# The opening stretch of a planned SSD and mixer kernel: the words of its first quarter in another order

## The chip, the core and the metric

The kernel runs on one core of one Trainium2 chip. The metric is the device time of one execution in microseconds (us), the median of several runs; for the kernel before the change it is 217.03 us (three runs, 217.02 to 217.46).

## What is computed

First a state space scan (Mamba2 SSD), over 4 batches of 8 heads with 768 tokens, 32 values a token and 16 state values, in chunks:

```python
for c in range(nc):
    cum = np.cumsum(log_a[:, :, sl], axis=-1)
    M = einsum('bhin,bhjn->bhij', Cc, Bc) * exp(cum_i - cum_j) * causal
    y[:, :, sl] = einsum('bhij,bhjd->bhid', M, xc) + einsum('bhin,bhnd->bhid', Cc, state) * exp(cum)
    state = decay_full * state + sum_j Bc_j * xc_j * decay_from_j
```

Then, for each batch, a mixer on the scan's output x (768 tokens by 256 channels):

```python
u = x + (x.T @ U @ V).T          # U: 768x32, V: 32x768
out = u + relu(u @ w_ch1) @ w_ch2   # 256 -> 1024 -> 256
```

U, V, w_ch1 and w_ch2 arrive as 64-bit numbers and are made 32-bit floats on the chip.

## The kernel before

All work is cut into small steps, and a string, PLANS (lines 36 to 71), says in which order they are recorded. Each step is a word: a letter for the kind of step, and numbers for its place. `follow` (lines 1070 to 1089) reads the words one by one and calls the step's function, and each engine then carries out its instructions in just that order. An engine never passes over a waiting instruction to a later one, so the order of the words is the order of TensorE (PE), VectorE (DVE), ScalarE (ACT), GpSimd (POOL) and of the load queue on SyncE (SP). PLANS[0] loads the first scan inputs; PLANS[1] holds everything else, for all four batches.

**The scan** works on pairs of 128-token blocks, three pairs a batch, twelve in all. In a word of PLANS[1] the pair number counts from batch 1: -3, -2 and -1 are the pairs of batch 0, 0 to 2 of batch 1, 3 to 5 of batch 2, and so on. The words of one pair k, in the order in which they depend on each other:

- B and X load B, C and x of a pair (L loads both). Q (one block) or P (the whole pair) multiplies B and C by decay factors on DVE (`prep`, 471). E or D makes the decayed B for the state (`decayed`, 483; on POOL for batch 0, else on DVE).
- V or T transposes that on PE and copies it out on ACT and DVE (`turning`, 494).
- g multiplies C by B on PE (`gram`, 583). It takes four banks of PSUM, two with the tag x and two with z. m and M apply the causal mask on DVE, for two banks each (`mask`, 597), and so free them.
- s makes what the pair adds to the state, on PE (`state`, 616); it takes the two banks with the tag w, which are free again when u has read them. u carries the state on, four small operations on DVE (`update`, 632), and then a masked copy on POOL or ACT.
- i and j multiply C by the carried state, and n the masked product by x, both on PE (`inter`, 699, and `intra`, 734). For batch 0, j may need a copy of one column on DVE, named settled (666), which waits for the products of i and n recorded before it. y copies the result out on ACT, t and O turn it back to tokens.

**The weights.** Z loads V and U. w0 and w1 load the two halves of the first quarter of w_ch1, w2 to w4 the other quarters, and w5 to w8 the quarters of w_ch2. c makes floats of such a load in three steps with one word each (`to_fp32`, 409): two operations on DVE and one on ACT, one on ACT, three on DVE. c0 is for U and V, c1 and c2 for w0 and w1, c3 to c9 for w2 to w8. R splits a quarter for the later, finer products (`refine`, 447), on ACT and DVE. v spreads U and V on PE and ACT (`spread`, 1012).

**The mixer.** p multiplies the scan's output by U, x by V (four banks at once, x and z), and a.0 and a.1 add the result to the scan's output on DVE, one half of the tokens each. For the first two of the three 256-token blocks of batch 0, products are plain: U1.j.i multiplies block j by quarter i of w_ch1, eight PE instructions (the profile shows 32-bit matmuls as two rows each) and a relu on ACT (`plain`, 864), and four words d1.j multiply by w_ch2 (`down`, 937). U1.0.0 needs a1.0, c1 and c2; U1.j.1 needs c3, and so on up to c5; the first d word of a block needs c6 and c7, the second c8 and c9. The third block and all later batches use the split numbers: S splits the input, f and e multiply by the first weights, h and d follow. f1.2.0 is the first such product.

**What sets the order of loads.** All loads are issued on SP, one after the other, and each of the words B, X, w and L is held until the last DVE operation recorded before it is done (`hold`, 197, and line 1075). A load into a buffer that is used again also waits for its last reader.

F sets how many filler products PE runs at the next bank. There are two PSUM banks with the tag w, three with x and three with z (line 130).

Of the kernel before, what the change touches and what calls it, by code (L numbers as in the profile page):

```python
# [70 lines left out]
}


# [1049 lines left out]
```

## Time and profile before

| | us |
|---|---|
| median of three runs | 217.03 |
| the profiled execution | 214.85 |
| its span, first to last instruction | 213.1 |
| PE busy | 202.6 |
| DVE busy | 172.9 |
| ACT busy | 121.3 |

The prediction sums against the profiled execution; its time is the span and 1.75 us around it. A row of a timeline gives the start, the duration, engine, line, operation, tiles and how many instructions are merged in it, and in brackets the idle time of the engine before it with what ended that. "issue" is idle time for which the profile shows no releaser. Times in the trace run from the start of the span. All DVE instructions carry the line 177 of a helper that records them; they are told apart by their tiles (BC is of P and Q, M of m and M, S of u, words, w1f and o of c, yT of a). On PE, line 853 is a product of the mixer, 591 g, 626 s, 721 i and j, 746 n.

### The profile page before, as it was taken

Reading aid. Unit: us, or ns where it says so; the run is one execution under the profiler, and the core shown is the slowest. Engines: PE = TensorE matmul, PEld = TensorE weight load, DVE = VectorE, ACT = ScalarE, POOL = GpSimd, SP = SyncE. Lnnn points to the kernel's source line nnn. Section 1 sums busy time; section 2 is a strip of 40 time slices with the busy share of each in tenths; the row PEclk is TensorE's granted clock in tenths of the full one; section 3 lists DMA queues with packets and bytes.
Section 4 is the critical chain, followed back from the end, with each engine's and each line's share of the span. In section 5 each row is a group of like instructions: output and inputs, shape, how many; then the busy total and the mean of one; then the engine's idle time right before and its main releaser. Section 6 shows DMA issues by size and latency. Waiting matters only on the chain.

```text
span 213.1 us, 7527 instructions
## 1 busy us (share of the span) xinstructions
PE 202.6 (95%) x3198; PEld 180.3 (85%) x3198; DVE 172.9 (81%) x363; ACT 121.3 (57%) x279; POOL 6.4 (3%) x22
## 2 busy tenths in 40 slices
PE   7979889979999999999999999899999999999994
PEld 4756666758879997988999999589998999999993
DVE  4588979989799999999899995777985299859941
ACT  3454678388969855186488441669713565554310
POOL 4131000000000000000000000000000000000000
DMA  6998899992752488346665756535510000314344
GB/s 90 120 144 183 97 254 226 229 161 90 101 67 35 74 203 125 100 64 95 89 109 102 172 114 145 95 53 89 135 53 0 0 5 0 49 31 73 52 98 98
DMA packets 120177, 21.43 MB, mean 101 GB/s; under 512 B 110096, under 2 KB 118352, under 8 KB 120144
## 3 DMA queue, kind: packets, MB, share of 16 engines
q1 hardware_dynamic: 120144, 20.95, 54.7%
q8 instruction: 25, 0.41, 0.9%
q14 instruction: 8, 0.07, 0.1%
HBM read 14.39 MB, written 6.55 MB: 98 GB/s over the span
## 4 chain that ended last, share of the span: by engine, by line
PE 77%; DVE 8%; issue 5%; DMA 3%; ACT 3%; SPq 1%; POOL 1%; POOLq 0%; DVEq 0%; ACTq 0%
PE x L853 34%; PE z L853 26%; DVE words L177 2%; DMA bc<-in_B_dram 2%; PE w L626 2%; PE x L591 2%; PE x L139 1%; PE w L810 1%; DVE S L177 1%; PE z L746 1%; PE x L746 1%; DMA ytok<-squares 1%; PE x L822 1%; PE x L721 1%; DVE o L177 1%
## 5 line engine op out<-in xcount | busy, mean ns | idle before, releaser
L177 DVE SCALAR_TENSOR_TENSOR words<-words 128x512 fp32r<-128x512 f32 (+6 forms) x60 | 39.2, 668 | 2.8 <-ACT words L427 1.4
L853 PE MATMUL x<-words,w 128*128 128x256 f32 x288 | 38.0, 280 | 0.1
L853 PEld LDWEIGHTS x<-words,w 128*128 128x128 f32 x288 | 34.9, 188 | 1.8 <-issue 1.2
L853 PE MATMUL x<-u,w 128*128 128x256 f32 x240 | 34.3, 282 | 0.0
L853 PE MATMUL z<-u,w 128*128 128x256 f32 x240 | 32.7, 278 | 0.0
L858 ACT ACTIVATE x<-x 128x512 f32<-128x512 f32 (+1 forms) x27 | 15.5, 577 | 29.5 <-PE x L853 27.8
L853 PEld LDWEIGHTS x<-u,w 128*128 128x128 f32 x240 | 30.4, 188 | 0.6 <-ACT yT L766 0.2
L853 PEld LDWEIGHTS z<-u,w 128*128 128x128 f32 x240 | 29.8, 188 | 0.1
L858 ACT ACTIVATE z<-z 128x512 f32<-128x512 f32 (+1 forms) x24 | 13.7, 574 | 12.4 <-PE z L853 10.3
L853 PE MATMUL z<-words,w 128*128 128x256 f32 x144 | 19.6, 280 | 0.0
L853 PEld LDWEIGHTS z<-words,w 128*128 128x128 f32 x144 | 17.7, 188 | 0.9 <-issue 0.9
L177 DVE SCALAR_TENSOR_TENSOR words<-x,words 128x512 fp32r<-128x512 f32 x20 | 13.6, 682 | 4.5 <-ACT words L893 4.4
L177 DVE SCALAR_TENSOR_TENSOR words<-z,words 128x512 fp32r<-128x512 f32 x20 | 13.6, 682 | 2.2 <-ACT words L893 2.2
L177 DVE SCALAR_TENSOR_TENSOR S<-S,kept,w 128x64 f32<-128x64 f32 x40 | 11.2, 279 | 3.5 <-PE w L626 2.0
L893 ACT ACTIVATE words<-x 128x512 fp32r<-128x512 f32 x20 | 12.0, 599 | 3.3 <-PE x L853 3.2
L177 DVE TENSOR_TENSOR yT<-x,yT 128x384 f32<-128x384 f32 (+1 forms) x15 | 9.2, 614 | 5.2 <-PE x L853 2.6
L893 ACT ACTIVATE words<-z 128x512 fp32r<-128x512 f32 x20 | 11.8, 598 | 1.9 <-PE x L853 1.2
L591 PE MATMUL x<-Cm,T 32*64 32x128 f32 x192 | 12.2, 308 | 0.4 <-DVE Cm L177 0.3
L658 ACT ACTIVATE Sm<-S,slot 128x128 f32<-128x128 f32 (+1 forms) x18 | 5.9, 385 | 10.8 <-DVE S L177 10.8
L177 DVE TENSOR_TENSOR BC<-bc,F 128x512 f32<-128x512 f32 (+2 forms) x18 | 8.6, 506 | 2.6 <-ACT F L379 1.3
L591 PE MATMUL z<-Cm,T 32*64 32x128 f32 x192 | 10.7, 307 | 0.0
L177 DVE TENSOR_TENSOR M<-x,causal 128x256 int32<-128x256 int32 x24 | 9.0, 418 | 1.6 <-PE z L591 1.6
(154 smaller groups left out, 363.6 us busy)
## 6 DMA issues: line engine op xcount, KB each, us to landing
words<-in_moe_w_ch_dram SPq DMA_DIRECT2D x7, 512.0 KB, 5.3
squares<-w1f SPq DMA_DIRECT2D x52, 64.0 KB, 2.0
x<-in_x_dram SPq DMA_DIRECT2D x24, 128.0 KB, 4.1
out_dram<-o SPq DMA_DIRECT2D x32, 64.0 KB, 2.2
bc<-in_B_dram SPq DMA_DIRECT2D x24, 64.0 KB, 3.4
bc<-in_C_dram SPq DMA_DIRECT2D x12, 128.0 KB, 3.6
T<-squares SPq DMA_DIRECT2D x6, 256.0 KB, 3.9
ytok<-squares SPq DMA_DIRECT2D x6, 256.0 KB, 3.0
```

What stands on the lines that cost most here:

```text
L139: nc.tensor.matmul(out=t[:, :m * w].rearrange("p (m i) -> p m i", i=w), lhsT=ident, rhs=ident[:, None, :w].to_broadcast([P, m, w]), start= ...
L177: self.last = call(*args, **kwargs)
L591: nc.tensor.matmul(out=g[r][cols, c], lhsT=s["T"][rows, 0, c, cols], rhs=s["Cm"][rows, :, :, ts(2 * c + p, Q)].rearrange("r v t i -> r v i ...
L626: nc.tensor.matmul(out=s["A"][p][ts(r, Q), v], lhsT=s["bd"][half, v, 2 * r:2 * r + 2].rearrange("p h n -> p (h n)"), rhs=x_sb[k][half, v, ...
L658: nc.scalar.activation(s["Sm"][:, sl, v], s["S"][:, sl, ts(v, D)], AF.Copy, scale=slot[:, v, None])
L721: product = nc.tensor.matmul(out=y[r // 2][p][ts(v, H), c], lhsT=own[ts(r, Q)], rhs=s["T"][ts(r, Q), 1, :, ts(2 * c + p, Q)].rearrange("r ...
L746: product = nc.tensor.matmul(out=y[n][p][ts(v, Q), c], lhsT=x_sb[k][half, c, h], rhs=s["M"][half, h // 2, c, h % 2], start=fresh(k, n, p, ...
L810: nc.tensor.matmul(out=p[ts(n, H)], lhsT=UU[:, c].rearrange("p t r -> p (t r)"), rhs=ytok[b][:, c, ts(n, P)], start=(c == 0), stop=(c == N ...
L822: nc.tensor.matmul(out=h[q][:, :VS], lhsT=pT[rows], rhs=V4[rows], start=True, stop=True, skip_group_check=True)
L853: nc.tensor.matmul(out=t, lhsT=lhsT, rhs=rhs, start=start, stop=True, skip_group_check=True)
L858: nc.scalar.activation(t, t, AF.Copy, scale=1.0 + EPS)
L893: nc.scalar.activation(gs[j, i][0], t, AF.Relu, scale=NEAR)
```

## The change

Only the string PLANS[1] changes, from its first word to "P4 T3 d1.0 f1.2.0"; that is about the first quarter of the words. The same words stand there in another order (a word such as T0 or c3 that occurs several times runs the next part of its step each time). Behind that point both strings agree. The diff, cut there:

```diff
 1: (
-        'Z1 F2 A0 Q-3.0 Q-3.1 A1 Q-3.2 F2 V-3.0.0 V-3.1.5 K2 D-3 g-3 Q-2.1 Q-2.2 Q-2.0 F0.8 V-2.0.2 Z0 '
-        'm-3 M-3 F2 V-2.1.2 Q-1.2 E-1.0 s-3 Q-1.0 D-2 n-3 w0 Q-1.1 V-1.0.2 u-3 F1 V-1.1.3 s-2 w1 i-3 '
-        'g-2 u-2 j-3 y-3 F2 g-1 i-2 B3 B4 B5 w2 w3 X3 w4 X4 m-2 M-2 w5 c0 c0 m-1 B6 O-3.0 c0 M-1 w6 '
-        'E-1.1 n-2 s-1 u-1 c2 v0 w7 c1 c2 j-2 i-1 y-2 j-1 n-1 c1 y-1 P0 D0 c1 T0 c2 t-2 O-1.3 P2 X5 '
-        'T0 X6 w8 P1 D2 p1.0.4 p1.4.6 c3 c3 x1 a1.0 a1.1 T1 T2 T2 T1 g0 U1.0.0 c3 c4 c4 U1.0.1 g1 m0 '
-        'M0 c5 c4 m1 M1 c5 D1 s0 u0 U1.1.0 U1.1.1 U1.1.2 i0 n0 y0 c6 c6 s1 c5 g2 c7 u1 R2 m2 c7 '
-        'U1.1.3 M2 c8 c8 c7 U1.0.2 L4 U1.0.3 i1 n1 y1 c6 R1 R0 c8 R5 c9 s2 c9 c9 n2 d1.0 L5 R6 u2 R0 '
-        'd1.1 P3 S1.2 d1.0 R7 d1.0 i2 y2 R3 t1 R1 t0 R2 R5 d1.1 R4 P4 T3 d1.0 f1.2.0 R4 T4 f1.2.2 t2 '
-        'e1.2.0 f1.2.1 R6 d1.0 d1.1 D3 R3 h1.2.0 P5 d1.1 e1.2.2 f1.2.3 e1.2.1 p0 T3 d1.2 e1.2.3 T4 '
+        'F2 A0 Z1 Z0 A1 Q-3.0 w0 Q-3.1 Q-3.2 F2 V-3.0.0 V-3.1.5 K2 D-3 Q-2.1 g-3 Q-2.2 s-3 Q-2.0 w1 '
+        'B3 B4 D-2 w2 F0.8 V-2.0.2 m-3 M-3 F2 V-2.1.2 u-3 Q-1.2 n-3 Q-1.0 B5 w3 g-2 Q-1.1 s-2 E-1.0 '
+        'm-2 E-1.1 M-2 V-1.0.2 i-3 j-3 s-1 u-2 c0 i-2 c0 u-1 F1 V-1.1.3 y-3 n-2 F2 g-1 j-2 c1 X3 c2 '
+        'c0 c1 y-2 m-1 c2 w6 i-1 t-2 O-3.0 M-1 j-1 w4 P0 v0 D0 P1 D1 n-1 y-1 T0 T0 c2 c3 T1 O-1.3 '
+        'p1.0.4 T1 w5 X4 c3 c1 g0 P2 p1.4.6 m0 T2 w8 M0 R0 c4 x1 T2 a1.0 U1.0.0 c4 a1.1 s0 g1 U1.1.0 '
+        'c3 c7 X5 c4 u0 c7 m1 w7 U1.0.1 M1 c7 U1.1.2 c5 L4 i0 c5 D2 n0 y0 c6 U1.1.1 U1.0.2 c6 R2 B6 '
+        'g2 c5 s1 m2 M2 u1 U1.1.3 t0 c8 U1.0.3 c9 s2 c6 R5 c8 R1 u2 c9 i1 n1 c8 d1.1 y1 d1.0 L5 c9 '
+        'S1.2 t1 R6 R2 n2 i2 P3 R0 d1.1 y2 X6 R7 d1.0 R5 R4 R3 d1.0 R1 P4 T3 d1.0 f1.2.0 R4 T4 '
+        'f1.2.2 t2 e1.2.0 f1.2.1 R6 d1.0 d1.1 D3 R3 h1.2.0 P5 d1.1 e1.2.2 f1.2.3 e1.2.1 p0 T3 d1.2 '
+        'e1.2.3 T4 T5 L6 h1.2.2 h1.2.1 R7 d1.1 x0 a0.0 a0.1 d1.2 h1.2.3 d1.2 d1.2 d1.2 s3 g3 m3 M3 '
 ...
```

In the new order

- s-3 follows g-3 at once, and g-2, s-2, m-2, M-2, s-1 and u-1 come before more of the conversions; the masks m0 and M0 of batch 1 come before a1.0;
- P0, P1 and P2 stand in this order (before: P0, P2, P1), and D2 comes later than D1;
- g0 stands ahead of p1.4.6 and x1, and U1.0.0 right behind a1.0; between the plain products U stand s0 and g1, then i0 and n0, then g2 and s1, t0, and s2, i1 and n1; d1.1 and d1.0 come ahead of n2 and i2;
- c7 comes ahead of c5, c6 behind it;
- the loads are issued in the order Z1 Z0 w0 w1 B3 B4 w2 B5 w3 X3 w6 w4 w5 X4 w8 X5 w7 L4 B6 L5 X6; before it was Z1 Z0 w0 w1 B3 B4 B5 w2 w3 X3 w4 X4 w5 B6 w6 w7 X5 X6 w8 L4 L5.

No instruction's size changes. On DVE, POOL and SP the same operations are issued, in another order and with some waits in other places.

43 rows, old and new, of the table PLANS are left out of this document.

## The prediction

> **What bounds the kernel now.** I read the shares first, then busy time by stage, then the rows of PE where the two orders meet again. Stage rows give the length, then busy time of PE, PEld, DVE, ACT and POOL, clock, DMA share and GB/s.
>
> ```profile
> span 213.1 us, 7527 instructions
> ...
> PE 202.6 (95%) x3198; PEld 180.3 (85%) x3198; DVE 172.9 (81%) x363; ACT 121.3 (57%) x279; POOL 6.4 (3%) x22
> ...
> q8 instruction: 25, 0.41, 0.9%
> ```
> ```profile
> 12.00:33.54 21.54, 18.83 (x548) 13.64 (x546) 18.34 (x55) 13.71 (x38) 2.71 (x5) 1.00 0.94 172
> 33.54:67.64 34.10, 32.61 (x557) 26.75 (x553) 31.14 (x69) 25.85 (x61) 0.00 (x0) 1.00 0.69 134
> 67.64:213.10 145.46, 141.44 (x2014) 132.84 (x2012) 117.18 (x218) 77.44 (x173) 0.00 (x0) 1.00 0.44 81
> ```
>
> The cuts are the first product of U1.0.0 (33.54) and of f1.2.0 (67.64). From f1.2.0 on both orders have the same words, and PE is busy for 141.44 of 145.46 us there: what PE gains or loses up to f1.2.0 should arrive at the end nearly whole. So the question is when PE reaches f1.2.0. The clock is 1.00 and plays no part.
>
> Ahead of 33.54 no engine is full: DVE is busy for 18.34 of 21.54 us, and the DMA share is 0.94. From 33.54 to 67.64 PE looks nearly full, but its rows show time that its words don't need:
>
> ```profile
> 33.54 1.99 PE L853 MATMUL x<-yT,w1f 128*128 128x256 f32 x8
> 35.69 1.99 PE L853 MATMUL z<-yT,w1f 128*128 128x256 f32 x8 [0.15 <-DVE w1f L177]
> ...
> 40.66 1.89 PE L853 MATMUL z<-yT,w1f 128*128 128x256 f32 x8
> 42.39 1.89 PE L853 MATMUL x<-yT,w1f 128*128 128x256 f32 x8
> ...
> 45.33 0.49 PE L626 MATMUL w<-x,bd 64*32 64x64 f32 x30
> 46.98 0.27 PE L626 MATMUL w<-x,bd 64*32 64x64 f32 x2 [1.16 <-issue]
> ...
> 59.00 1.03 PE L853 MATMUL x<-words,o 128*128 128x256 f32 x4
> 60.20 2.86 PE L853 MATMUL x<-words,o 128*128 128x256 f32 x12 [0.17 <-DVE o L177]
> 62.99 0.28 PE L721 MATMUL x<-T,Sm 32*64 32x64 f32 x2
> ```
>
> A product word of 8 rows takes 42.39 - 40.66 = 1.73 us from start to start. Against that U1.0.0 lost 0.42 (35.69 - 33.54 = 2.15), waiting for the next quarter of w1 (c3); s1 lost 1.4 (45.33 to 47.18, 1.85, for 0.45 of work); the two d words from 59.00 lost 0.53 (3.99 to 62.99, for 3.46), waiting for c9. With 0.15 of small refills that is 2.5 of the 34.10 us: **what PE has to do there is 31.6 us.**
>
> The "issue" wait of 1.16 us has no releaser, and it has a twin earlier:
>
> ```profile
> 16.11 0.30 PE L626 MATMUL w<-x,bd 64*32 64x64 f32 x4 [1.16 <-issue]
> ```
> ```profile
> 16.11:21.03 4.92, 4.51 (x127) 3.19 (x127) 4.32 (x14) 2.00 (x5) 0.97 (x2) 1.00 0.88 188
> 21.03:25.07 4.04, 3.50 (x128) 2.57 (x128) 3.90 (x13) 3.03 (x10) 0.51 (x1) 1.00 0.79 89
> 25.07:31.71 6.64, 6.03 (x129) 4.72 (x127) 5.29 (x14) 4.20 (x11) 0.00 (x0) 1.00 1.02 227
> 31.71:41.96 10.25, 10.10 (x130) 7.44 (x129) 10.18 (x25) 6.53 (x13) 0.00 (x0) 1.00 0.94 214
> 41.96:46.98 5.02, 3.86 (x129) 3.07 (x128) 4.34 (x12) 3.80 (x12) 0.00 (x0) 1.00 1.11 209
> ```
>
> From the first pause to the second lie 643 PE and 639 PEld rows, 1282, or five blocks of 256; and 3198 + 3198 rows over the 25 instruction packets of the page is 256 as well. So I read both pauses as PE waiting for its next 256 instructions. Blocks of small scan products take 4 to 5 us and run into the edge; the one with most plain products takes 10.25 and does not.
>
> **The change, part by part.** *DVE up to a1.0.* U1.0.0 needs yT of word a1.0. Up to M-3's masks, which end at 12.38, DVE has the same work in both orders; a1.0 starts at 31.76 now.
>
> ```profile
> 12.38:31.76 19.38, 16.67 (x513) 12.62 (x512) 16.18 (x51) 11.55 (x32) 2.71 (x5) 1.00 0.96 173
> ```
> ```profile
> 10.31 0.82 DVE L177 TENSOR_TENSOR BC<-bc,F 128x128 f32<-128x128 f32 x3
> ...
> 16.45 0.91 DVE L177 SCALAR_TENSOR_TENSOR S<-S,kept,w 128x64 f32<-128x64 f32 x3 [1.19 <-PE w L626]
> ...
> 29.54 1.29 DVE L177 TENSOR_TENSOR BC<-bc,F 128x512 f32<-128x512 f32 x2 [1.28 <-DMA bc<-in_B_dram]
> ...
> 31.76 0.55 DVE L177 TENSOR_TENSOR yT<-x,yT 128x384 f32<-128x384 f32 x1
> ...
> 33.62 1.28 DVE L177 SCALAR_TENSOR_TENSOR words<-words 128x512 f32<-128x512 f32 x2
> 34.94 0.69 DVE L177 SCALAR_TENSOR_TENSOR w1f<-words 128x512 f32<-128x512 f32 x1
> 35.55 0.76 DVE L177 TENSOR_SCALAR words<-words 128x512 int32<-128x512 int32 x2
> 36.22 0.75 DVE L177 TENSOR_TENSOR M<-x,causal 128x256 int32<-128x256 int32 x2
> 36.89 0.75 DVE L177 TENSOR_TENSOR M<-z,causal 128x256 int32<-128x256 int32 x2
> ```
>
> Of 19.38 us 3.2 are idle. The wait of 1.19 for s-2 goes: the new order has m-2 and M-2 (1.33, as 36.22 to 37.55) ahead of u-2, and they fill it, although the same block edge still falls into s-2. The 1.28 goes: P2, which waits for the last load of B, no longer stands ahead of P1, D1 and the ends of c1 and c2. Added ahead of a1.0 are the four masks of pair 0 (1.33) and c4's first step (0.67, 35.55 to 36.22); D1 comes in place of D2. Without idle, a1.0 would start at 12.38 + 16.18 + 2.0 = 30.6. New waits: c0 needs U, which is issued as now and lands at 17.6 (below), while DVE is there at 17.0: 0.6. The second "settled" copy now waits for n-2, which lies at the next edge (0.3, an estimate by the 4.92 of a block). That makes 31.5.
>
> *Loads.* P2 and c4 need B3, B4, w2, B5 and w3, now and then; only w2 moves ahead of B5.
>
> ```profile
> 13.65 1.51 SPq L203 DMA_DIRECT2D words<-in_moe_U_dram  x1
> 15.28 0.99 SPq L203 DMA_DIRECT2D words<-in_moe_w_ch_dram  x2
> ...
> 25.44 1.20 SPq L203 DMA_DIRECT2D words<-in_moe_w_ch_dram  x2
> ```
> ```profile
> SPq L203 <- DVE settled L177: 1.1, 1, 1.1
> ```
> ```profile
> words<-in_moe_U_dram SPq DMA_DIRECT2D x1, 192.0 KB, 3.9
> ```
> ```profile
> words<-in_moe_w_ch_dram SPq DMA_DIRECT2D x2, 512.0 KB, 5.6
> ```
>
> The last row is w2 and w3, issued from 25.44 to 26.64 and landed in 5.6 in the middle, w3 at about 32.2. The 1.1 that SP waits for a "settled" copy before B3 goes, because B3 now follows a DVE word that ends at 11.13 (row 10.31). So w3 lands between 31.0 and 32.2; I take 31.1, as the wait was SP's own, and c4's first step ends at 31.8. **a1.0 starts at 31.8, and U1.0.0, with g0 done ahead of it, after a1.0's two operations at 32.9 instead of 33.54**; bounds 31.7 (loads and waits cost nothing) and 34.0 (w3 at 32.2). X4, X5, B6 and X6 go later on SP, and L4 and L5 ahead of X6; X6 is issued behind R0, near 62, and lands some 4 us later; its reader s3 is PE's at 83.27 (the other row is for the next part):
>
> ```profile
> 31.76:60.10 28.34, 26.95 (x519) 21.24 (x516) 25.63 (x60) 21.38 (x48) 0.00 (x0) 1.00 0.74 153
> ```
> ```profile
> 83.27 0.46 PE L626 MATMUL w<-x,bd 64*32 64x64 f32 x32
> ```
>
> So I cost that at nothing; without this cover of 15 us, s3 would wait out the landing. ACT's R0 and c7 come earlier; ACT is busy for 25.85 of 34.10 us and takes them in.
>
> *PE from U1.0.0 to f1.2.0.* The words are the same, 31.6. Two more returns from scan to product words cost a refill of 0.1 each: 0.2. The 1.4 at s1 goes: counted in the new order, edges fall into U1.1.2, g2, n1 and n2, and each block behind them has two product words or more (3.5 us). The 0.42 goes: U1.0.1 comes behind s0, g1 and U1.1.0, at 37.6, and c3 (2.0 us, 33.62 to 35.63) ends at 35.7. The 0.53 goes: DVE now works 25.63 us from a1.0 to c9's end (31.76:60.10); less the 2.0 already done, with u2 (0.8) and a wait of 1.1 for g2, c9 ends at 31.8 + 25.5 = 57.3, and PE comes to it at 58.5. New waits: U1.1.2 takes the bank that m1 frees. DVE is there behind c3, c7's first step, c4 and u0, at 35.7 + 0.67 + 1.95 + 1.1 + 0.67 = 40.1, PE at 39.4: 0.6. t0 takes a bank that u1 frees, behind g2, m2 and M2 at 49.7, PE is there at 49.4: 0.3. What queues behind both on PE (i0 and n0; U1.0.3 and s2) is late by that and counted with it.
>
> Sum: 32.9 + 31.6 + 0.2 + 0.6 + 0.3 = 65.6 against 67.64, **2.0 us sooner**. DVE ends T3, the last common point, some 3 us sooner, so it doesn't become the bound behind it.
>
> [...]
>
> **The rivals.** *Loads bind.* The five loads land no sooner, w3 at 32.2; a1.0 at 33.0, U1.0.0 at 34.0, the sum 66.7: 0.9 gained, 216.1. For it: the DMA share of 0.94. Against: 0.79 at 21.03:25.07.
>
> *The pause stays, or comes back elsewhere.* 65.6 + 1.4 = 67.0: 0.6 gained, 216.4. For it: the three scans of batch 0 still stand close up to n-1, and g2 beside s1. Against: the block of 10.25 us, which mixes both kinds, has no pause. With both rivals nothing is gained.
>
> *Slower: DVE is late at a1.0.* The order puts 2.0 us more on DVE ahead of a1.0. If the 3.2 us of idle stay in another form (copies and masks waiting for scan words behind edges, 4 to 5 us a block), a1.0 is at 31.76 + 2.0 + 0.7 for c4's step behind w3 = 34.5, U1.0.0 at 35.6, and with 31.6 and 1.1 behind it f1.2.0 is at 68.3: 0.6 slower, 217.6. It decides when over 2 us of the idle stay.
>
> **How the numbers follow.** The profiled execution took 214.85 us, 1.75 more than its span; less 2.0 that is 212.85. The median of the runs shown is 217.03, 2.2 above it; I take the same 2.0 from it: **215.0**. Chances: forecast 0.46, loads 0.14, pause 0.11, both together (nothing gained) 0.09, slower 0.20. A measurement of this kernel can tell about 0.2% (0.43 us) from no change: the first three cases are faster, less 0.02 at their edge, 0.69; same 0.11; slower 0.20. The range reaches from U1.0.0 at 31.7 with one of the new waits gone (1.2 + 0.3 sooner, 213.5) to the slower rival: 213.5 to 217.7.
>
> **What would show it.** Right: U1.0.0's first product near 32.9 and f1.2.0's near 65.6, no "issue" wait over 0.5 us on PE between, and no DVE wait for in_B over 0.5 at P2. Wrong: a1.0 later than 33.5; a new "issue" wait at g-1, n-1 or g2; U1.1.3 or d words waiting for c5 to c9; or a gain at f1.2.0 that is not there at the end, by which the common part isn't PE's.

## The result and the profile after

The changed kernel takes 218.90 us (median of 20 executions, 216.74 to 221.49) against 216.28 for the kernel before on the same chip (20 executions, 213.53 to 218.77): 1.014 times as long, 95% interval 1.0107 to 1.0173. This ratio and all ratios below leave out executions in a slower state (three of the 20 here), so they are not the quotients of the medians. The prediction had 215.0, and a range that ended at 217.7. The profiled execution took 218.26 us.

The page of the changed kernel; the third row is the granted clock in 40 slices of the span:

```profile
span 216.6 us, 7528 instructions
...
PE 205.9 (95%) x3198; PEld 182.0 (84%) x3198; DVE 174.1 (80%) x363; ACT 120.5 (56%) x279; POOL 6.5 (3%) x22
...
PEclk9996559999999999999999999999999999999999
```

PE's instructions are the same number, but 3.3 us more of busy time, and a clock row, which the page of before did not have, shows slices at 6, 5, 5 and 6 tenths. The shares don't say more; the stages do. The rows below go from the end of M-3's masks to a1.0 on DVE, then the two parts of PE that the prediction had cut (columns as before):

```profile
12.53:37.68 25.15, 21.93 (x512) 15.72 (x512) 18.61 (x56) 13.91 (x37) 2.66 (x5) 0.73 0.83 168
38.30:71.33 33.03, 32.82 (x553) 26.64 (x553) 31.68 (x67) 24.88 (x60) 0.00 (x0) 1.00 0.62 117
71.33:216.60 145.27, 141.17 (x2014) 132.62 (x2012) 116.06 (x216) 76.69 (x172) 0.00 (x0) 1.00 0.44 82
```

U1.0.0's first product is at 38.30 instead of 33.54, 4.8 us late, and f1.2.0's at 71.33, 3.7 late. So the second part gave back 1.1 us (33.03 for 34.10), the common part is what it was (145.27 for 145.46), and the whole loss lies ahead of U1.0.0. There DVE was busy for 18.61 us and idle for 6.54; it had been idle for 3.2. The DVE rows with their waits:

```profile
19.94 0.63 DVE L177 TENSOR_SCALAR words<-words 128x384 int32<-128x384 int32 x2 [2.20 <-DMA words<-in_moe_U_dram]
...
30.01 0.76 DVE L177 TENSOR_SCALAR words<-words 128x512 int32<-128x512 int32 x2 [0.46 <-DMA words<-in_moe_w_ch_dram]
33.16 0.42 DVE L177 COPY ytok<-z 128x256 f32<-128x256 f32 x1 [2.39 <-PE z L776]
...
35.59 0.76 DVE L177 TENSOR_TENSOR M<-x,causal 128x256 int32<-128x256 int32 x2 [0.27 <-PE z L591]
...
37.68 0.56 DVE L177 TENSOR_TENSOR yT<-x,yT 128x384 f32<-128x384 f32 x1
```

They are c0's first step, which waits 2.20 us for U; c3's first step, which waits for w2; the copy of T1, which waits 2.39 us for a product of PE; pair 0's masks; and a1.0. Why PE was late at the copy is seen in stretches of the clock, which in this trace is 1.00 or 0.50 and changes only at 18.22, 31.88 and 216.20 us, four and 54 times 3.41 us apart (column after POOL's):

```profile
14.81:18.22 3.41, 1.97 (x63) 1.35 (x50) 2.83 (x10) 0.90 (x3) 1.00 (x3) 1.00 0.97 218
18.22:21.64 3.42, 3.23 (x92) 2.50 (x84) 1.62 (x7) 1.07 (x2) 0.38 (x2) 0.50 0.77 154
21.64:25.05 3.41, 2.62 (x50) 1.90 (x50) 2.89 (x11) 1.97 (x6) 0.34 (x1) 0.50 0.46 48
25.05:28.46 3.41, 3.05 (x29) 2.38 (x24) 3.16 (x9) 1.64 (x4) 0.00 (x0) 0.50 0.87 169
28.46:31.88 3.42, 3.42 (x98) 2.28 (x98) 1.82 (x5) 1.65 (x5) 0.00 (x0) 0.50 0.88 145
```

PE is busy for 1.97 of 3.41 us, and the next four stretches run at half the clock, 13.7 us in all. After the one with 3.42 busy the clock is back. The mean clocks of the 20 executions lie between 0.96 and 0.992, so each of them lost at least one such stretch.

The loads are late too. U was issued at 14.61 and landed at 19.85, not at 17.6; the median from issue to landing, and the code packets that the DMA engines moved from 17.0 to 17.6 us:

```profile
words<-in_moe_U_dram SPq DMA_DIRECT2D x1, 192.0 KB, 5.2
```
```profile
q8 instruction: 1, 0.02, 9.7%
```

And w3 landed at 34.34, after 32.17 before. The rows of SP around it are w2, B5 and w3:

```profile
24.78 1.01 SPq L203 DMA_DIRECT2D words<-in_moe_w_ch_dram  x1
25.90 0.40 SPq L203 DMA_DIRECT2D bc<-in_B_dram  x1
26.35 0.58 SPq L203 DMA_DIRECT2D bc<-in_C_dram  x1
26.97 2.81 SPq L203 DMA_DIRECT2D bc<-in_B_dram  x1
29.83 0.58 SPq L203 DMA_DIRECT2D words<-in_moe_w_ch_dram  x1
```

The third load of B5 takes 2.81 us to issue, and w3 stands behind it.

### The profile page after: what moved, and what is told of

It is laid out like the page before. It is cut to its first block, busy times and chain, and to the rows that moved or that the text cites. A ratio compares the mean times of both kernels' runs of the same rounds, so it can differ in the third digit from the quotient of the medians.

```text
span 216.6 us, 7528 instructions
## 1 busy us (share of the span) xinstructions
PE 205.9 (95%) x3198; PEld 182.0 (84%) x3198; DVE 174.1 (80%) x363; ACT 120.5 (56%) x279; POOL 6.5 (3%) x22
## 4 chain that ended last, share of the span: by engine, by line
PE 78%; SPq 6%; DVE 5%; ACT 4%; DMA 2%; issue 2%; DVEq 0%; ACTq 0%
PE x L853 36%; PE z L853 26%; SPq L203 6%; PE x L591 3%; DMA words<-in_moe_U_dram 2%; PE x L746 1%; DVE M L177 1%; PE w L810 1%; PE z L746 1%; PE x L721 1%; DVE words L177 1%; PE x L822 1%; DVE S L177 1%; ACT yT L766 1%; PE w L776 1%
## 5 line engine op out<-in xcount | busy, mean ns | idle before, releaser
L853 PE MATMUL x<-u,w 128*128 128x256 f32 x240 | 34.3, 282 | 0.0
L177 DVE SCALAR_TENSOR_TENSOR words<-x,words 128x512 fp32r<-128x512 f32 x20 | 13.7, 683 | 4.5 <-ACT words L893 4.4
L591 PE MATMUL x<-Cm,T 32*64 32x128 f32 x192 | 11.3, 317 | 0.6 <-DVE Cm L177 0.3
L177 DVE TENSOR_TENSOR BC<-bc,F 128x512 f32<-128x512 f32 (+2 forms) x18 | 9.8, 564 | 1.2 <-ACT F L379 0.6
L591 PE MATMUL z<-Cm,T 32*64 32x128 f32 x192 | 10.2, 316 | 0.0
```

What stands on the lines that cost most here:

```text
L177: self.last = call(*args, **kwargs)
L591: nc.tensor.matmul(out=g[r][cols, c], lhsT=s["T"][rows, 0, c, cols], rhs=s["Cm"][rows, :, :, ts(2 * c + p, Q)].rearrange("r v t i -> r v i ...
L853: nc.tensor.matmul(out=t, lhsT=lhsT, rhs=rhs, start=start, stop=True, skip_group_check=True)
```

## The experiments

The theory after the result: the thin PE work of the new opening lets the clock fall, and U, a load that lands late, holds DVE. The rival: the order itself has too much waiting for DVE ahead of a1.0, and neither repair would bring the forecast.

**c0 later.** Only the words are moved:

```diff
-s-1 u-2 c0 i-2 c0 u-1 F1 V-1.1.3 y-3 n-2 F2 g-1 j-2 c1 X3 c2
+s-1 u-2 i-2 u-1 F1 V-1.1.3 y-3 n-2 F2 g-1 j-2 c0 c0 c1 X3 c2
```

> The new order with one edit: the first two words of c0 (U and V made floats) go from between u-2 and u-1 to behind j-2, just ahead of c1. Theory 1 (the conversion of U, placed ahead of u-1, lets DVE, and behind it PE, wait 2.2 us for U's load; the thin work on PE in that stretch drops the granted clock to 0.50 for 13.7 us): the wait for U on DVE falls below 0.5 us, the clock stays near 1.00, U1.0.0 starts near 33 instead of 38.3, and the time is 1 to 2 us below that of the kernel before. Theory 2 (the loads of the new order come late whatever stands where): U1.0.0 still starts at 36 or later and the kernel stays slower than before by 1 us or more.

Measured: 1.0112 (1.0022 to 1.0203). The wait for U is gone, a1.0 starts at 35.13 and U1.0.0 at 35.73, 2.6 us sooner than in the changed kernel, and f1.2.0 33.0 us later as there. The clock still falls, for two stretches instead of four; the stretch ahead of it and the first of them:

```profile
14.20:17.60 3.40, 2.44 (x85) 1.41 (x66) 3.33 (x11) 0.90 (x3) 1.48 (x3) 1.00 0.80 161
17.60:21.00 3.40, 3.06 (x79) 2.47 (x80) 1.58 (x7) 0.00 (x0) 1.12 (x2) 0.50 0.96 210
```

So U is not the cause of the clock, and the loss is not U alone.

**More filler.** Eight idle products more for PE:

```diff
-m-2 E-1.1 M-2 V-1.0.2 i-3 j-3 s-1 u-2
+m-2 E-1.1 M-2 F4 V-1.0.2 i-3 j-3 F4 s-1 u-2
```

> The new order with filler products only: F4 ahead of V-1.0.2 and F4 ahead of s-1, in the stretch from 14.8 to 18.2 us in which PE was busy for 1.97 of 3.41 us before the clock fell. The wait for U stays. Theory 1a (the clock is what costs, the wait for U is cheap by itself): the clock stays at 1.00, U1.0.0 starts near 35 and f1.2.0 near 68, about the time of the kernel before, within 0.5 us. Theory 1b (the wait is what costs, and the lower clock is only hidden under it): the clock is back at 1.00 but U1.0.0 stays at 37 or later and the time within 0.5 us of the new order's.

Measured: 1.0075 (1.0030 to 1.0120); the mean clock of its nine timed executions is 0.997 to 1.000. The products compute nothing and cost PE time (F2 at 11.67 us of the changed kernel took 0.70 us), and the kernel is faster with them: the clock is a cause, worth about half of the 1.4%, with an interval of 0.3 to 0.45% on either ratio. The profiled execution was the longest of the ten (218.85 us, mean clock 0.992) and does not decide between the two expectations: U1.0.0 is at 37.73 there, and DVE waits 1.4 us for U, 1.7 for w2 and 1.2 for a load of B.

**The old order with less filler.** From the kernel before, F1 ahead of V-1.1.3 and F2 ahead of g-1 are taken out:

```diff
-Q-1.1 V-1.0.2 u-3 F1 V-1.1.3 s-2 w1 i-3 g-2 u-2 j-3 y-3 F2 g-1
+Q-1.1 V-1.0.2 u-3 V-1.1.3 s-2 w1 i-3 g-2 u-2 j-3 y-3 g-1
```

> The kernel before with two fillers taken out (F1 ahead of V-1.1.3 and F2 ahead of g-1); its order is unchanged. If thin work on PE near 15 to 18 us is what drops the clock, this kernel drops it too: granted clock 0.50 for one to four stretches of 3.4 us, U1.0.0 at 35 to 38, 1.5 to 4 us slower than the kernel before. If the drop belongs to something else in the new order, the clock stays at 1.00 and the time is the same or up to 0.7 us shorter.

Measured: 1.0052 (1.0000 to 1.0103). In its profile the clock falls twice, each time behind a stretch with little PE work:

```profile
13.70:17.10 3.40, 1.69 (x47) 1.07 (x45) 1.64 (x6) 1.28 (x4) 0.84 (x2) 1.00 0.91 191
17.10:20.50 3.40, 3.19 (x91) 2.94 (x95) 2.83 (x10) 1.30 (x4) 0.97 (x2) 0.50 0.65 150
44.40:47.80 3.40, 2.20 (x124) 1.56 (x123) 3.18 (x9) 3.30 (x11) 0.00 (x0) 1.00 0.93 166
47.80:51.20 3.40, 3.29 (x35) 2.59 (x35) 2.14 (x8) 2.84 (x6) 0.00 (x0) 0.51 0.89 193
```

U1.0.0 is at 33.88, 0.3 us late and not at 35 to 38; the stretch from there to f1.2.0, with the second fall in it, takes 35.9 us for 34.1. The old order stands near the same edge, and its fillers make the fall rarer: 7 of the 10 executions here have a mean clock of 0.984 or less, 5 of the 19 of the kernel before beside it.

**U ahead of V.**

```diff
-F2 A0 Z1 Z0 A1 Q-3.0
+F2 A0 Z0 Z1 A1 Q-3.0
```

> The changed kernel with U loaded ahead of V (Z0 Z1 for Z1 Z0), nothing else. In it U landed at 19.85 us, 4.8 us after its issue, and its last 63 packets of 256 B came 1.0 to 1.6 us behind the others; one 16 KB packet of the instruction queue started at 17.11, among them. Theory (the code packet holds up the part of U that shares its DMA engine): one place earlier in the queue U's packets are done before 17.1, U lands by 17.3, the wait of 2.2 us for U goes, V lands late instead and nobody waits for it, and U1.0.0 comes at 35.5 to 36.5 instead of 38.30; the granted clock still falls to 0.50 near 18 us, so the kernel stays slower than before, by 0.5 to 1.2%. Rival (the new order's loads are late as such, by SP's issue): U lands at 19 or later in either place, and the ratio stays at 1.014.

Measured: 1.0070 (1.0017 to 1.0123), U1.0.0 at 35.63, in the expected 35.5 to 36.5. The medians to landing, and DVE's wait:

```profile
words<-in_moe_U_dram SPq DMA_DIRECT2D x1, 192.0 KB, 3.4
words<-in_moe_V_dram SPq DMA_DIRECT2D x1, 192.0 KB, 4.6
```
```profile
DVE words L177 <- DMA words<-in_moe_V_dram: 1.4, 1, 1.4
```

U is in early, but c0's first step reads both, which the expectation had missed, so a wait of 1.4 us for V takes the place of 2.2 for U. The clock is low for two stretches here, not for four, so part of the 2.7 us by which U1.0.0 comes sooner is the clock's. The packets of the trace show which load is late. In the changed kernel nine tenths of U's 768 packets had started by 17.50 and the last at 19.12, with a 16 KB code packet from 17.11 to 18.04; in the kernel before, with code packets at 13.24 and 18.42, these were 16.83 and 17.17. With U first its last packet started at 16.93, the code packet at 16.83, and V has the tail (17.38, then 18.66). In the five profiles with V ahead of U and a code packet that began between 16.4 and 17.8 us, the last tenth of U's packets trailed by 1.3 to 1.8 us; in the two in which no code packet overlapped V's or U's, by 0.2 and 0.3. This fits packets that wait behind the code packet, but no run moved the code packet alone, so it is read from the traces, not shown by an edit.

**U ahead of V, and the eight products.** Both edits above.

> Both repairs of the changed kernel at once: U ahead of V, and four idle products (F4) ahead of V-1.0.2 and four ahead of s-1, as in the run with more filler. Theory (the clock and U are the whole loss ahead of U1.0.0): the clock stays at 1.00, no wait for U, U1.0.0 at 32.9 to 34.0 and f1.2.0 33.0 us later, at 66 to 67; the ratio to before is 0.990 to 1.000. Rival (the rest lies in the new order itself, DVE's added masks and c4's step or the later weights): U1.0.0 stays at 35 or later with the clock at 1.00, and the ratio is 1.003 or more.

Measured: 1.0009 (0.9967 to 1.0052). The clock row of the page, and all of DVE's listed waits ahead of a1.0:

```profile
PEclk9999999999999999999999999999999999999999
```
```profile
DVE words L177 <- DMA words<-in_moe_V_dram: 1.2, 1, 1.2
DVE words L177 <- DMA words<-in_moe_w_ch_dram: 1.0, 2, 0.7
DVE BC L177 <- DMA bc<-in_C_dram: 1.0, 1, 1.0
DVE settled L177 <- PE z L721: 0.9, 1, 0.9
```

With a full clock, and a wait of 1.2 us for V in place of 2.2 for U, no loss clear of noise is left in the ratio; but nothing of the forecast gain is there either, and the profile still shows a loss. U1.0.0 is at 36.12, not at 33 to 34, and f1.2.0 at 69.16, 1.5 us behind the profile of the kernel before; in the changed kernel it was 3.7 behind. So the two repairs take back over half, and the first theory explains most of why the kernel was slower, and not why it was not faster.

**Filler in the old order.** Four products ahead of V-1.0.2, and four instead of one ahead of V-1.1.3:

```diff
-Q-1.1 V-1.0.2 u-3 F1 V-1.1.3
+Q-1.1 F4 V-1.0.2 u-3 F4 V-1.1.3
```

> The kernel before with four idle products ahead of V-1.0.2 and four instead of one ahead of V-1.1.3. Several executions of the kernel before had a mean clock of 0.982 to 0.992, that is one or two stretches of 3.41 us at half clock. Theory (those come from the thin PE work near 15 us too): clock near 1.00 in all executions, ratio 0.993 to 1.000. Rival (they fall elsewhere, near 48 us as in the run with less filler, or by chance): the same clocks as before and a ratio of 1.000 to 1.005, the idle products costing a little.

Measured: 0.9994 (0.9949 to 1.0039). The mean clocks are 0.991 to 1.000, those of before beside it 0.984 to 1.000: fewer lost stretches, and no time that can be told from nothing.

**The old opening with the new second half.** Before's words up to g0, then the new ones (D1, m0, M0 and c4's first step now ahead of U1.0.0, the words that the opening already holds left out):

```diff
-x1 a1.0 a1.1 T1 T2 T2 T1 g0 U1.0.0 c3 c4 c4 U1.0.1 g1 m0
+x1 a1.0 a1.1 T1 T2 T2 T1 g0 D1 m0 M0 R0 c4 U1.0.0 c4 s0 g1 U1.1.0 c3
...
```

> The kernel before up to and with g0; from there all remaining words in the new order (masks m0 and M0 and c4's first step ahead of U1.0.0, then products and scan words alternately). In the new order's own profile the stretch from U1.0.0 to f1.2.0 took 33.0 us against 34.1 before. If that half of the change is a gain by itself, U1.0.0 starts near 33.5, no issue wait over 0.5 us follows it, f1.2.0 starts near 66.5 and the kernel is 0.8 to 1.5 us faster than before. If the gain was only made because everything ahead of it was late (loads and conversions had longer to finish), the stretch takes 34 us again and the time is that of the kernel before within 0.4 us.

Measured: 1.0469 (1.0381 to 1.0557). It tells nothing of the alternation: the new half converts w6 ahead of w4, the old opening loads it behind w5 and B6, and DVE waited 3.5 us for it in one piece. The loads were then put in the order of their use:

```diff
-B3 B4 B5 w2 w3 X3 w4 X4 m-2 M-2 w5 c0 c0 m-1 B6 O-3.0 c0 M-1 w6
+B3 B4 B5 w2 w3 X3 w6 X4 m-2 M-2 w4 c0 c0 m-1 B6 O-3.0 c0 M-1 w5
```

> The earlier run with the old words up to g0 and the new words behind them again, with the loads w4, w5 and w6 permuted to w6, w4, w5, the order in which the new words convert them. There VectorE waited 4.0 us for a weight load and f1.2.0 came 41.3 us after U1.0.0. Theory (the alternating half is a gain by itself, 33.0 us from U1.0.0 to f1.2.0 in the changed kernel against 34.1 before, and the earlier run lost it to the load order alone): no wait for w6, U1.0.0 near 35.4 (it now stands behind the masks of pair 0 and c4's first step, 1.9 us), f1.2.0 at 68 to 69, and a ratio of 0.995 to 1.006. Rival (the alternating half needs the scans of the new first half, or lighter loads, beside it): f1.2.0 36 us or more after U1.0.0, ratio above 1.01.

Measured: 1.0112 (1.0057 to 1.0168), 36.4 us from U1.0.0 to f1.2.0. The weights come in time; now DVE waits 2.35 us at D1, whose buffer s0 releases, and s0 stands behind U1.0.0. D1 was moved behind u0:

```diff
-g0 D1 m0 M0 R0 c4 U1.0.0 c4 s0 g1 U1.1.0 c3 c7 c4 u0 c7 m1
+g0 m0 M0 R0 c4 U1.0.0 c4 s0 g1 U1.1.0 c3 c7 c4 u0 D1 c7 m1
```

> The old words up to g0 and the new ones behind, with the loads permuted, and D1 moved from ahead of m0 to behind u0. In the run without that move VectorE waited 2.35 us at D1 for the scan word s0, which releases its buffer, and TensorE then 1.04 and 0.72 us for VectorE. Theory (the alternating half is a gain by itself of about 1 us, 33.0 for 34.1): no such wait, U1.0.0 near 33.4, f1.2.0 at 66.5 to 68.0, ratio 0.992 to 1.000. Rival (the gain needs weights that are already in: w4 and w5 land later against it, as the first product comes 5 us sooner than in the changed kernel): f1.2.0 at 68.5 or later, with waits for c7, c5 or c8, ratio above 1.000.

Measured: 1.0050 (1.0016 to 1.0085); from U1.0.0 (35.03) to f1.2.0 (69.30) it takes 34.3 us, as in the kernel before (34.1), and not the 33.0 of the changed one. So the alternating half is no gain by itself behind the old opening. The row of that stretch:

```profile
35.03:69.30 34.27, 33.61 (x557) 26.94 (x553) 32.52 (x71) 26.13 (x63) 0.00 (x0) 1.00 0.68 139
```

Where the 1.2 us lie can be read from the rows of both profiles. U1.1.1 starts 10.9 us behind U1.0.0 here and 9.7 in the changed kernel, and from there to f1.2.0 both take 23.3. Here DVE does m0, M0 and c4's first step behind the start of U1.0.0, there it has done them ahead of a1.0; so the last mask of M1 ends 9.5 us behind U1.0.0 here and 8.4 there, and n0 starts at 10.1 and 8.9. The gain of the second part is thus in the main DVE's work that was done, and paid for, in the first. No edit tests this for the masks; for c4's step two runs below do.

**Three repairs, and two.** What was left looked like w3: with c0 later, and with U ahead of V and the eight products, a1.0 followed its landing by 0.7 us. So c0 later, the eight products, and w2 behind B5 as before, once with the last edit and once without:

```diff
-B3 B4 D-2 w2 F0.8
+B3 B4 D-2 F0.8
...
-Q-1.0 B5 w3 g-2
+Q-1.0 B5 w2 w3 g-2
```

> The changed kernel with three repairs: c0's two steps behind j-2 (U is in by then), eight idle products more (F4 ahead of V-1.0.2 and of s-1; the clock stays at 1.00), and w2 loaded behind B5 as before, next to w3. In the four kernels with the changed first half and no wait for U or a full clock, a1.0 started 0.2 to 0.7 us after w3 had landed, at 34.3 to 34.8 us, against 32.2 in the kernel before; there the third load of B5, behind w2, takes 2.6 to 3.2 us to issue, and w3 is issued only after it. Theory (w3 is what is left of the loss ahead of U1.0.0, and the place of w2 is why it is late): w3 lands at 32 to 33, a1.0 starts at 32.5 to 33.5, U1.0.0 at 33.2 to 34.2, f1.2.0 33 us later, and the ratio to before is 0.992 to 1.000. Rival (w3 is late because the loads as a whole are, the DMA share being 0.83 against 0.96, or the work of VectorE binds by itself): a1.0 at 34.5 or later, ratio above 1.000.

> The same with w2 left where the change put it, ahead of B5: the control. Theory: clock 1.00, no wait for U, w3 at 34.3 to 35, a1.0 at 35 to 35.6, U1.0.0 near 36 and the ratio 1.000 to 1.005, as with U ahead of V and the idle products. Rival (U alone had bound, c0 later gives more than U ahead of V did): a1.0 before 34 with w3 landing earlier too, ratio below 1.000.

Measured: 1.0106 (1.0067 to 1.0144) with w2 behind B5, 1.0086 (1.0041 to 1.0132) without. Both miss. In both profiles the clock falls after all, at 27.3 and at 25.0 us: with c0 moved, the thin stretch of PE comes later. And in the first, a1.0 is at 36.59 though w3 is in at 33.38; there c3's step waits 1.7 us for w2. That w3 was all that was left is refuted.

**w2 behind B5, with U ahead of V and the products.** The same edit where the clock is safe:

> The run with U ahead of V and eight idle products more (clock 1.00, ratio 1.0009), and one edit beside it: w2 loaded behind B5 as in the kernel before, so that w2 and w3 are issued one after the other. There w3 landed at 34.81 us and a1.0 started at 35.51, right behind c4's first step, which reads w3. Theory (there w3 is what still binds a1.0, and part of its lateness is the place of w2): w3 lands at 32.5 to 33.5, a1.0 starts 1 to 2 us sooner, U1.0.0 at 34.2 to 35.2, f1.2.0 33.0 us later, ratio 0.993 to 1.000. Rival (VectorE's other waits, for the scans and for w2, which now comes later, take up what w3 gives): w3 sooner but a1.0 at 35 or later, ratio 1.000 to 1.006.

Measured: 1.0070 (1.0041 to 1.0100), against 1.0009 without the edit. That difference, between two chips, is not shown to be the edit's: f1.2.0 is at 69.20 with it and at 69.16 without. w3 landed at 32.26, 2.5 us sooner, and a1.0 started at 35.55, as without. DVE's rows say why:

```profile
28.42 0.42 DVE L177 SCALAR_TENSOR_TENSOR w1f<-words 128x256 f32<-128x256 f32 x1
30.82 0.76 DVE L177 TENSOR_SCALAR words<-words 128x512 int32<-128x512 int32 x2 [1.98 <-DMA words<-in_moe_w_ch_dram]
...
34.89 0.75 DVE L177 TENSOR_SCALAR words<-words 128x512 int32<-128x512 int32 x2
35.55 0.55 DVE L177 TENSOR_TENSOR yT<-x,yT 128x384 f32<-128x384 f32 x1
```

c3's first step (30.82) waits 1.98 us for w2, which now lands at 30.79, and from there DVE works without a gap to a1.0: 4.73 us, c3's step itself, the copy of T1, c1's rest, P2, pair 0's masks and c4's step. In the old order 0.67 us lie between c3's step and a1.0. So the new order has two bounds on a1.0 through the loads, w2 + 4.7 and w3 + 0.7, and SP's order only trades one for the other: 30.35 + 4.7 or 34.81 + 0.7 with w2 first, 30.79 + 4.7 or 32.26 + 0.7 with w2 behind B5.

**c3 later, and c4 too.** To the last kernel, c3's first two steps behind M0, and then c4's first step behind a1.1:

```diff
-T0 T0 c2 c3 T1 O-1.3 p1.0.4 T1 w5 X4 c3 c1 g0 P2 p1.4.6 m0 T2 w8 M0 R0 c4 x1 T2 a1.0 U1.0.0 c4 a1.1
+T0 T0 c2 T1 O-1.3 p1.0.4 T1 w5 X4 c1 g0 P2 p1.4.6 m0 T2 w8 M0 R0 c3 c3 c4 x1 T2 a1.0 U1.0.0 c4 a1.1
...
+T0 T0 c2 T1 O-1.3 p1.0.4 T1 w5 X4 c1 g0 P2 p1.4.6 m0 T2 w8 M0 R0 c3 c3 x1 T2 a1.0 U1.0.0 a1.1 c4 c4
```

> The run with w2 behind B5 (full clock, ratio 1.007), and c3's first two steps moved from ahead of T1 to behind M0, next to c4's first step. In that run VectorE waited 1.98 us for w2 and then worked without a gap from 30.82 to a1.0 at 35.55. Theory (c3's place is what makes w2 bind): the copy of T1, c1's rest, P2 and the masks of pair 0, 3.4 us, are done while w2 comes; a1.0 starts at 33.2 to 34.0, U1.0.0 at 33.8 to 34.6, f1.2.0 33.0 us later, ratio 0.994 to 1.001. Rival (VectorE's work is too much whatever the order): a1.0 at 35 or later, ratio 1.004 or more.

> The same with c4's first step behind a1.1 as well, where the kernel before has it, so that no step ahead of a1.0 reads w3. Theory: a1.0 another 0.6 us sooner, 32.6 to 33.4, U1.0.0 at 33.2 to 34.0; U1.0.1 then waits up to 0.7 us for c3's end, so that f1.2.0 comes 33.0 to 33.7 us later; ratio 0.992 to 1.000. Rival: as with c3 alone, 1.004 or more.

Measured: 1.0064 (1.0027 to 1.0102) and 1.0044 (1.0003 to 1.0085); a1.0 at 34.94 and 34.36, 0.6 and 1.2 us sooner than in the run with c3 early. None of w0 to w3 is waited for any more, the clock is full, and a1.0 is still 2.6 us later than before. In the second one DVE is busy for 17.70 us from M-3's masks (12.70) to a1.0 and idle for 3.96. Its waits:

```profile
DVE ytok L177 <- PE z L776: 1.4, 1, 1.4
DVE words L177 <- DMA words<-in_moe_V_dram: 1.0, 1, 1.0
DVE settled L177 <- PE z L721: 0.9, 1, 0.9
DVE settled L177 <- PE z L746: 0.2, 1, 0.2
```

The copy of T1 now comes before its product is done, V is still a little late, and the two settled copies wait for scan products. Of the latter, the 0.9 us is a price of the idle products, four of which stand ahead of i-3: this wait is in all seven profiles with them and in none of the three with the new opening and without. Both theories were half right: c3's place holds a1.0 up, but by 0.6 us and not by 1.5 to 2.4, and behind it other waits stand. The other 0.6, of c4's step, is no gain at all. From U1.0.0 to f1.2.0 the second kernel takes

```profile
34.97:68.53 33.56, 33.35 (x553) 26.82 (x553) 32.36 (x69) 25.53 (x61) 0.00 (x0) 1.00 0.70 135
```

and the first 33.04 us, so that f1.2.0 is at 68.53 and 68.58: DVE's step is paid for on either side of a1.0.

**c3 early in the old order.** The reverse test, one step moved in the kernel before:

```diff
-P0 D0 c1 T0 c2 t-2 O-1.3 P2 X5 T0 X6 w8 P1 D2 p1.0.4 p1.4.6 c3 c3 x1 a1.0
+P0 D0 c1 c3 T0 c2 t-2 O-1.3 P2 X5 T0 X6 w8 P1 D2 p1.0.4 p1.4.6 c3 x1 a1.0
```

> The kernel before with one edit: c3's first step moved from ahead of x1 to ahead of T0, that is ahead of the copy of T0, c2's rest, P2, P1 and D2. w2 landed at 30.7 there. Theory (a step that waits for w2 holds up all VectorE work behind it): VectorE waits some 3 us for w2, the 1.28 us for the last load of B go, and a1.0 starts at 33.8 to 34.6 instead of 31.76; ratio 1.008 to 1.014. Rival (the loads do not bind VectorE through c3): a1.0 within 0.5 us of 31.8, ratio 0.998 to 1.003.

Measured: 1.0211 (1.0147 to 1.0274), more than either theory said. c3's step and a1.0:

```profile
31.16 0.76 DVE L177 TENSOR_SCALAR words<-words 128x512 int32<-128x512 int32 x2 [4.22 <-DMA words<-in_moe_w_ch_dram]
...
36.46 0.56 DVE L177 TENSOR_TENSOR yT<-x,yT 128x384 f32<-128x384 f32 x1 [1.54 <-PE z L822]
```

DVE stands 4.22 us for w2, PE waits 3.5 us for a copy behind it, and behind a stretch with PE that idle the clock is at half from 30.9 to 41.1 us (its mean over the execution is 0.977). One step of 0.67 us, put ahead of work that does not need it, costs 2.1%, against 1.4% for the whole change, though the two intervals overlap. About half of the 5.2 us by which f1.2.0 is late (72.85) goes with the slow PE, an estimate from two rows: a1.0 waits 1.54 us for it, and U1.0.0 comes 2.9 us behind a1.0 instead of 1.8.

## Why the prediction was wrong

**The step that failed is "DVE up to a1.0".** It took DVE's work as 16.18 + 2.0 = 18.2 us, and 18.61 was measured. The waits that were to go did go: no product of a scan word for S makes DVE wait 1.19 us, and P2 (34.63) does not wait for B. But beside the work the step had 1.2 us of idle time (0.6 for U, 0.3 for a settled copy, 0.3 for w3), and 6.54 was there. Three terms make up 5.8 us of it:

- U, 0.6 in the sum, cost 2.20. "Issued as now and lands at 17.6" failed on the landing: issued at 14.61 it landed at 19.85. Moving c0's step off it, and U in the queue, each brought a1.0 forward by over 2 us, though with two stretches of low clock fewer as well.
- The clock, 0 in the sum ("1.00 and plays no part"). It was read from one execution of the old order, and others of that order do lose stretches (mean clocks of 0.984 to 1.000 beside the run with more filler in the old order). The new order puts scan steps that wait for DVE side by side, PE is busy for 1.97 us of one stretch, and a mask of pair -1, the copy of T1 and a mask of pair 0 wait 0.48, 2.39 and 0.27 us for a PE that is at half speed or late from it. Filler alone brought the ratio from 1.014 to 1.0075, and with the same order of c3 and T1 and a full clock (U ahead of V, and the products) the copy does not wait.
- w2, 0 in the sum. The loads were checked for P2 and c4, and c3's step, which waits for w2 in the new order with 4.1 us of other DVE work behind it, was not. It cost 0.46 there, as the waits for U and PE had already made DVE late, and 1.98 in the run that showed it.

The settled copies were not the failing term: the changed kernel shows no wait of theirs, and with the products 0.2 us is left beside the 0.9 that the products cause.

**The loads themselves.** w3 was to land at 31.1, at worst at 32.2, and landed at 34.34. That "only w2 moves ahead of B5" was taken as free: the third load of B5 then took 2.81 us to issue, and w3 came behind it. With w2 behind B5 that load takes 0.58 us in the kernel before, and w3 lands 2.5 us sooner in the run with that edit (32.26 for 34.81). So even without the three waits a1.0, behind c4's step of 0.67, could not have come before 35.0 in the changed kernel, 3.2 us later than forecast. The rival that named the loads had this direction and 2.1 us too little.

**The slower rival** had the place right, "DVE is late at a1.0", and its point of decision held: over 2 us of the idle stayed. It did not have the causes: it put the idle time down to scan words behind block edges, and counted neither the clock nor the late U and w3. It had 0.20 of the chances and the price 217.6.

**What was right.** From U1.0.0 to f1.2.0 the prediction had 32.7 us (31.6 + 0.2 + 0.6 + 0.3), and 33.03 was measured; the common part behind it is unchanged, and no "issue" wait of PE over 0.3 us is left. The first is right in the sum rather than in its terms, by luck: PE was busy for 32.82 and idle for 0.2, not 31.8 and 0.9. What went is idle time, 1.5 us in the kernel before and 0.2 now; the rest of the 2.5 us that the prediction called lost was busy time, and PE's busy time did not shrink (32.61 before). U1.0.0 came 0.6 us behind a1.0's start instead of 1.1, which hides half a microsecond of the loss ahead of it. U1.0.0's row, the only one of PE with a wait that is listed from there to f1.2.0, waits for a1.0:

```profile
38.30 2.03 PE L853 MATMUL x<-yT,w1f 128*128 128x256 f32 x8 [0.26 <-DVE yT L177]
```

And the 1.1 us that this part gave could not be had behind the old opening.

**What stays open.** How much of the loss is clock and how much is U: filler alone takes back 0.65%, U's place alone 0.70%, both 1.3%, with intervals of 0.3 to 0.5% on each ratio. Two kernels with both repairs and f1.2.0 at the same time measured 1.0009 and 1.0070, so no finer split than that is shown. No kernel tried was faster than the kernel before by more than its interval; whether this order could be is not settled. The nearest, with c3 and c4 later, has f1.2.0 at 68.53 against 67.64, and 0.9 us of DVE's waits there come from the idle products that keep the clock up.

## What to carry to other kernels

In an engine that works in order, as DVE does here (it stood 4.22 us for w2 ahead of work that did not need it), ask for each step that waits for a load how much work behind it does not need that load, and where the load lands; the price of an early step is that work, not its own 0.67 us. Where a stage of TensorE is thin, its clock belongs into the sum: a reordering that leaves PE's work alone can still halve its speed for a while (13.7 us here). And a gain worked out from idle time that goes should be written down with the waits that come next, each with its own row, before it is added up.

## What the runs showed of the hardware

**The clock falls without a long gap.** In the 14 profiles that show a step of the clock, cut into its stretches of 3.41 us up to 60 us, about 200 stretches began at full clock. In 24 of them PE was busy for about 2.5 us or less, and the clock fell behind 11 of these; it fell behind none of the others. Rows of single profiles show it: ahead of a fall 1.97 us in the changed kernel, 2.44 with c0 later, 1.69 and 2.20 in the old order with less filler, 1.92 with two repairs (21.60 to 25.00); with the clock kept behind them, 2.11 in the changed kernel (7.98 to 11.40) and 2.25 with two repairs (14.80 to 18.20). The longest idle time of PE in the changed kernel's stretch from 14.81 was 0.65 us, between small scan products, and the clock fell behind that stretch. Little PE work in a stretch went with each of these falls, but does not decide alone, as 13 of the 24 kept the clock; what else decides is open.

**A code packet among a load's packets.** That PE's two waits of 1.16 us without a releaser in the kernel before are block edges was the author's estimate from counts of rows. In the changed kernel PE's longest such wait is 0.2 us, but one 16 KB packet stood among U's 768, and U's last packet started 1.6 us behind the first nine tenths (0.3 in the kernel before).

**The same products at two rates, with the clock granted in full.** From about 175 us to the end, where all 17 kernels have the same words, the rows of PE's mixer products start every 117.8 ns on average in seven profiles and every 113.5 in the other ten, the kernel before and the changed kernel among them, with a granted clock of 1.00 in both. From f1.2.0 to the end it takes 146.7 to 147.6 us in the seven and 144.6 to 145.7 in the ten (147.6 with c3 later, 145.1 with U ahead of V and the products). What decides it is open. So the end of a single profile does not tell two of these orders apart; the time of f1.2.0 and the ratios over many executions do.
